# Eight attention blocks and two gated MLPs on one core: the weight conversions of block 0 regrouped into pairs, with unread products ahead of it

## The chip, the cores and the metric

One core of one Trainium2 chip runs the whole program. The metric is device time in microseconds of one execution; the kernel before stands at 1517.81 us, the median of three runs (1516.03 to 1519.38).

## The reference

```python
def sm_attn(qq, kk, vv):                      # q, k, v: (8, 8, 576, 64); p: (8, 8, 32, 64)
    s = scale * np.matmul(qq, kk.transpose(0, 1, 3, 2))
    a = np.exp(s - np.max(s, axis=-1, keepdims=True))
    a = a / (np.sum(a, axis=-1, keepdims=True) + 1e-09)
    return np.matmul(a, vv)
p_packed = sm_attn(p, k, v)
x = sm_attn(q, p_packed, p_packed)            # -> (4608, 512), heads side by side
h = x @ w_in;   x = (h / (1 + exp(-h))) @ w_out
h = x @ w_in2;  out = (h * clip(h + 3, 0, 6) / 6) @ w_out2
```

All eight batch entries pass through both MLPs with 2048 hidden features. The four weight matrices arrive as float64.

## The kernel before, in words

**Blocks.** The first MLP runs in nine blocks of 512 tokens (`block`, L840): one for the first 512 rows of each batch entry, and a ninth (`j == B`) for the eight tails of 64 rows. Block j computes MLP 1 for its tokens, and beside it the attention of entry j+1. For 16 groups f of 128 hidden features `hidden` (L788) issues 6 products of 512 columns (operands in a high and a low half: high by high, high by low, low by high), then a Silu on ACT (L814), a copy of the high half on ACT (L821) and the low half on DVE (L822). `projects` (L853) issues 12 products of group f-2. So a block has 288 products, 18 per group. The second MLP follows, over five stretches of tokens; the change does not touch it.

**Fused input weights.** In blocks 0 to 7 the attention output is not formed: `fuse_products` (L580) multiplies the packed values by the input weights `wi[g]`, four groups f at a time, and `fuse_split` (L586) makes the halves on ACT (L590) and DVE (L593). `hidden` multiplies these by the turned attention weights (`high_u` L538, `low_u` L543). The tails' rows are formed apart: `step_ut` (L554) turns the weights of the tail on DVE and spreads them on POOL (L560), `step_xt` (L564) multiplies, `flush` stores.

**Float64 conversion.** The weights of the first MLP come in 32 units of 128 rows by 512 numbers, 16 of `w_in` and 16 of `w_out`, each a load of 512 KB (`load_raw`, L117). A unit costs ACT two scalings (`conv_a` L142, `conv_b` L148), DVE a shift and a sign step (L157, L161) and POOL an add (L171 or L173). Units of `w_out` also get a high half on ACT (L184) and a low half on DVE (L189); the odd ones are stored (`keep`, L176) and read again in later blocks. Class `Feed` (L1265) sets the order: four units ahead of block 0, two begun there, the others at two calls of `advance` per group f. Inside block 0 the loads are issued from ACT's queue, before that from SP's.

**Order around it.** Everything ahead of block 0 is written out by hand (L1338 to L1457): loads, attention of entry 0, its first units, the first fused products. Inside the blocks the class `Plan` (L600) places the steps of `attention` (L746): its clock `now` counts products, plus a cost for each step; a step runs when its place (share of the block's products) is reached, when the steps it needs are a given number of counts old (times 1.5 in block 0) and when banks of PSUM are free. `plan.finish` (L669) runs what is left over at once: at the start of a group that needs fused weights, at `boundary` (L1504, after product 264 of 288) and at the block's end. Each engine takes its instructions in program order.

Of the kernel before, what the change touches and what calls it, by code (L numbers as in the profile page):

```python
# [18 lines left out]
def tile_pack_attention_two_mlps(ctx: ExitStack, tc, q, k, v, p, w_in1, w_out1, w_in2, w_out2, out):  # L19
# [5 lines left out]
    P = 128  # L25
# [9 lines left out]
    RAW = 6  # L35
# [12 lines left out]
    gp = opened(first_left, "gp", bufs=3)  # L48
# [68 lines left out]
    def load_raw(key):  # L117
        if key[0] == "in":
            _, g, c = key
            src = w_in1.bitcast(I32)[c * P:(c + 1) * P, 2 * g * T:2 * (g + 1) * T]  # L120
        else:
            src = w_out1.bitcast(I32)[key[1] * P:(key[1] + 1) * P, :]
        raw = cv.tile([P, 2 * T], I32, tag="raw", name="raw", bufs=RAW)
        (load_queue[0] if early[0] else nc.scalar).dma_start(out=raw, in_=src)
        raws[key] = raw
# [10 lines left out]
    def ring():  # L136
        return cv.tile([P, T], F32, tag="ring", name="cr", bufs=8)

    def conv_a(key, room=ring):
        raw = raws.pop(key).rearrange("p (f t) -> p f t", t=2)  # L140
        r = room()
        nc.scalar.mul(out=r, in_=f32(raw[:, :, 1]), mul=2.0 ** -112)  # L142
        raws[key] = raw, r.bitcast(I32)

    def conv_b(key, room=ring):
        raw, r = raws.pop(key)
        t = room().bitcast(I32) if room is ring else raw[:, :, 0]
        nc.scalar.mul(out=t, in_=raw[:, :, 0].bitcast(U32), mul=2.0 ** -29)  # L148
        raws[key] = raw[:, :, 1], r, t
# [18 lines left out]
    def conv_add(key):  # L168
        r, t = raws.pop(key)
        if key[0] == "in":  # L170
            nc.gpsimd.tensor_add(out=wi[key[1]][:, key[2], :].bitcast(I32), in0=r, in1=t)  # L171
            return
# [3 lines left out]
    def keep(behind=2):  # L176

        while len(kept) > behind:
# [3 lines left out]
    def conv_hi(key):  # L182
        v, w = raws[key], half_w(key[1])
        nc.scalar.copy(out=w[:, 0], in_=v)  # L184
        made[key] = w

    def conv_lo(key):
        f, v, w = key[1], raws.pop(key), made[key]
        nc.vector.tensor_sub(out=w[:, 1], in0=v, in1=f32(w[:, 0]))  # L189
        if f % 2:  # L190
            kept.append((w1o[f].rearrange("n p f -> p n f"), f32(w)))

    def conv_end(key):
        conv_hi(key)
        conv_lo(key)
# [31 lines left out]
    class Prep:  # L227
# [31 lines left out]
        def all(self):  # L259
# [3 lines left out]
            for u, (kind, f, h) in enumerate(self.units):  # L263
                key = "p", u
                c = self.pool.tile([P, 8, P], F32, tag="c8", name="c8", bufs=2)
# [61 lines left out]
    def load_nat(b, what, c):  # L327
# [3 lines left out]
        if what == "v":  # L331
# [20 lines left out]
    def load_next():  # L352

        while loaded[0] < min(used[0] + 6, len(uses)):
# [18 lines left out]
    def turn(b, what, c, engine):  # L373
# [7 lines left out]
        turn_rows(ps, m)  # L381
# [171 lines left out]

    def step_ut(b):  # L554
# [31 lines left out]
    def fuse_split(b, g, to):  # L586
# [974 lines left out]
```

## Time and profile before

| | |
|---|---|
| median of three runs | 1517.81 us |
| the profiled execution | 1516.45 us, span 1514.7 us |
| TensorE (PE) busy, granted clock over the span | 1454.8 us (96%), 0.985 |
| DVE, ACT, POOL busy | 1011.8, 736.0, 187.3 us |
| first product of block 0 / of a projection / of block 1 | 43.04 / 59.74 / 172.90 us |
| DMA | 316.56 MB, mean 209 GB/s |

Busy times of matrix products overlap, since they are pipelined; starts in the timeline are the surer measure. A line `A <- B` in the view of waits says that A's engine sat idle and that B ended it.

### The profile page before, as it was taken

The numbers are of one execution on the slowest core, as the hardware profiler recorded it, in microseconds if no ns is written. First come the engines' busy times: TensorE is split into PE (matmuls) and PEld (weight loads), VectorE is DVE, ScalarE is ACT, GpSimd is POOL, SyncE is SP. The second block draws the span as 40 slices with busy tenths as digits, with TensorE's granted clock in tenths as the row PEclk, the third lists the DMA queues.
The fourth block names the chain that finished last, engine by engine and source line by source line (L and its number), as shares of the span: only waits on it lengthen the run. The fifth ranks groups of instructions, "written<-read, shape, count | busy, mean of one in ns | idle before, by whom it ended". The sixth has DMA issues, their size and how long they took to land.

```text
span 1514.7 us, 21753 instructions
## 1 busy us (share of the span) xinstructions
PE 1454.8 (96%) x7860; PEld 1167.6 (77%) x7860; DVE 1011.8 (67%) x1590; ACT 736.0 (49%) x1146; POOL 187.3 (12%) x150
## 2 busy tenths in 40 slices
PE   6688699999999999999999999999999999999998
PEld 3456467777777777777888888888888888999998
DVE  5666546565655655543682769786978687778767
ACT  4676346545465646545662344334443443444443
POOL 1333011111111121123240000000000000000000
PEclk9899899999999999999999999999999999999999
DMA  9567376857576576468983566577657766998887
GB/s 227 181 189 193 101 221 189 218 150 213 141 214 177 164 177 188 129 178 225 296 254 122 192 218 219 194 222 248 222 195 221 237 216 211 284 313 253 273 273 221
DMA packets 394186, 316.56 MB, mean 209 GB/s; under 512 B 189280, under 2 KB 291168, under 8 KB 393568
## 3 DMA queue, kind: packets, MB, share of 16 engines
q1 hardware_dynamic: 386328, 300.56, 67.6%
q10 hardware_dynamic: 7752, 14.62, 3.1%
q8 instruction: 63, 1.03, 0.3%
q14 instruction: 43, 0.35, 0.1%
HBM read 257.43 MB, written 57.67 MB: 208 GB/s over the span
## 4 chain that ended last, share of the span: by engine, by line
PE 86%; ACT 5%; DVE 4%; DMA 2%; issue 1%; POOL 1%; SPq 1%; ACTq 0%; POOLq 0%; DVEq 0%
PE acc L829 8%; PE b L1087 8%; PE b L1085 8%; PE b L1086 8%; PE b L1180 8%; PE b L1183 7%; PE acc L831 7%; PE b L1182 7%; PE acc L830 7%; PE hps L802 4%; PE hps L804 4%; PE hps L803 4%; PE abank L406 3%; DMA nat<-in_k_dram 1%; ACT hps L814 1%
## 5 line engine op out<-in xcount | busy, mean ns | idle before, releaser
L822 DVE TENSOR_TENSOR gl<-hps,gh 128x512 fp32r<-128x512 f32 x144 | 99.1, 688 | 221.3 <-ACT gh L821 221.1
L1183 PE MATMUL b<-ro,ws 128*128 128x512 f32 (+2 forms) x564 | 206.2, 366 | 0.0
L1182 PE MATMUL b<-ro,ws 128*128 128x512 f32 (+2 forms) x564 | 206.2, 366 | 0.0
L1085 PE MATMUL b<-xc,ws 128*128 128x512 f32 (+1 forms) x560 | 205.8, 367 | 0.0
L1087 PE MATMUL b<-xc,ws 128*128 128x512 f32 (+1 forms) x560 | 205.6, 367 | 0.0
L1086 PE MATMUL b<-xc,ws 128*128 128x512 f32 (+1 forms) x560 | 205.6, 367 | 0.0
L1128 DVE TENSOR_TENSOR ro<-g,ro 128x1024 fp32r<-128x1024 f32 (+1 forms) x140 | 161.2, 1156 | 42.1 <-ACT ro L1123 41.7
L1123 ACT CAST ro<-g 128x1024 fp32r<-128x1024 f32 (+1 forms) x140 | 131.8, 965 | 94.0 <-DVE g L1116 33.4
L814 ACT ACTIVATE hps<-hps 128x512 f32<-128x512 f32 x144 | 84.0, 584 | 154.4 <-PE hps L804 153.9
L1180 PE MATMUL b<-ro,ws 128*128 128x512 f32 (+2 forms) x564 | 139.0, 367 | 0.3
L829 PE MATMUL acc<-gh,wr 128*128 128x512 f32 x288 | 117.0, 406 | 8.0 <-ACT wr L184 8.0
L829 PE MATMUL acc<-gh,wo 128*128 128x512 f32 x288 | 117.2, 407 | 3.1 <-DMA wo<-w1o 3.0
L1183 PEld LDWEIGHTS b<-ro,ws 128*128 128x128 f32 x564 | 105.9, 188 | 13.2
L1182 PEld LDWEIGHTS b<-ro,ws 128*128 128x128 f32 x564 | 105.9, 188 | 13.1
L1085 PEld LDWEIGHTS b<-xc,ws 128*128 128x128 f32 x560 | 105.1, 188 | 13.5
L1086 PEld LDWEIGHTS b<-xc,ws 128*128 128x128 f32 x560 | 105.1, 188 | 13.2
L1087 PEld LDWEIGHTS b<-xc,ws 128*128 128x128 f32 x560 | 105.1, 188 | 13.1
L1180 PEld LDWEIGHTS b<-ro,ws 128*128 128x128 f32 x564 | 102.9, 188 | 15.1 <-DVE ro L1128 2.1
L802 PE MATMUL hps<-a2h,fused 128*128 128x512 f32 x256 | 107.0, 418 | 7.3 <-ACT fused L590 7.3
L831 PE MATMUL acc<-gh,wo 128*128 128x512 f32 x288 | 114.0, 396 | 0.1
L831 PE MATMUL acc<-gh,wr 128*128 128x512 f32 x288 | 113.5, 394 | 0.4 <-DVE wr L189 0.4
L830 PE MATMUL acc<-gl,wo 128*128 128x512 f32 x288 | 113.2, 393 | 0.0
(173 smaller groups left out, 2653.9 us busy)
## 6 DMA issues: line engine op xcount, KB each, us to landing
ws<-w2in SPq DMA_DIRECT2D x280, 256.0 KB, 3.2
ws<-w2out SPq DMA_DIRECT2D x280, 256.0 KB, 3.0
wo<-w1o SPq DMA_DIRECT2D x64, 512.0 KB, 4.5
x1d<-x SPq DMA_DIRECT2D x18, 512.0 KB, 3.8
praw<-in_moe_w_in_dram SPq DMA_DIRECT2D x32, 256.0 KB, 4.5
praw<-in_moe_w_out_dram SPq DMA_DIRECT2D x32, 256.0 KB, 4.5
raw<-in_moe_w_out_dram ACTq DMA_DIRECT2D x15, 512.0 KB, 3.6
nat<-in_v_dram SPq DMA_DIRECT2D x28, 256.0 KB, 3.2
```

Source lines behind the costliest of these rows:

```text
L802: mm(ps, lhsT=wh, rhs=rh, start=c == 0, stop=False)
L829: mm(acc[e], lhsT=w[:, 0, s], rhs=gh, start=first, stop=False)
L830: mm(acc[e], lhsT=w[:, 0, s], rhs=gl, start=False, stop=False)
L831: mm(acc[e], lhsT=w[:, 1, s], rhs=gh, start=False, stop=last)
L1085: mm(ps, lhsT=wh, rhs=xs[k][:, 0, c], start=first, stop=False, skip_group_check=True)
L1086: mm(ps, lhsT=wh, rhs=xs[k][:, 1, c], start=False, stop=False, skip_group_check=True)
L1087: mm(ps, lhsT=wl, rhs=xs[k][:, 0, c], start=False, stop=last, skip_group_check=True)
L1123: nc.scalar.copy(out=t[:, 0], in_=v)
L1128: nc.vector.tensor_sub(out=t[:, 1], in0=self.operand(s), in1=f32(t[:, 0]))
L1180: mm(to, lhsT=wh, rhs=x, start=False, stop=last, skip_group_check=True)
L1182: mm(to, lhsT=wh, rhs=x, start=first, stop=False, skip_group_check=True)
L1183: mm(to, lhsT=wl, rhs=x, start=False, stop=False, skip_group_check=True)
```

## The change

The diff below is cut; a line of "..." stands for lines left out.

1. Conversion units are taken in pairs (`raw` and `ring` tiles twice as wide, three `raw` buffers in place of six), so 16 pairs in place of 32 units; halves are still made one unit at a time. The loads go out on SP's queue throughout.
2. `Feed` gets a table: pair k starts at step `STARTS[k]`; its scalings, shift, sign, add and halves follow at steps +0, +1, +3, +4, +6, +9, +11, and at +6 the next load is asked for. Inside block 0 a step passes every 4.5 products. Steps below zero are issued ahead of block 0. The first loads of entry 1 move from ahead of block 0 to steps 1 to 9.
3. Ahead of block 0 the order is rewritten: entry 0's q is loaded ahead of v, in long rows, and turned by ordinary products; the softmax of the second attention takes the tail with it; 9, 8 and 20 products of 128 columns whose result nobody reads stand at three places (four of 512 columns before).
4. `attention`: waits are longer, `u` is cut in three steps, `exps` steps run only right after a group's Silu, `s` needs the `ut` of the entry before. At the end of blocks 0 to 5 `ut`, `xt` and `flush` may stay open into the next block. In block 0 places p become 0.1 + 0.84 p.

```diff
-    RAW = 6
+    RAW = 3
     def load_raw(key):
+        raw = cv.tile([P, 2, 2 * T], I32, tag="raw", name="raw", bufs=RAW)
+        for i in range(2):
...
-        (load_queue[0] if early[0] else nc.scalar).dma_start(out=raw, in_=src)
+            nc.sync.dma_start(out=raw[:, i], in_=src)
     def ring():
-        return cv.tile([P, T], F32, tag="ring", name="cr", bufs=8)
+        return cv.tile([P, 2, T], F32, tag="ring", name="cr", bufs=4)
+    def ring_low():
+        return gp.tile([P, 2, T], F32, tag="x1", name="ct", bufs=2)
...
     def turn(b, what, c, engine):
-        turn_rows(ps, m)
+        if b or what == "k":
+            turn_rows(ps, m)
+        else:
+            for i in range(NI):
+                for h in range(2):
+                    mm(ps[h * D:(h + 1) * D, i * P:(i + 1) * P], lhsT=m[:, h, i, :], rhs=ident, start=True, stop=True)
...
         def ready(self, key, need, tile, bank, count):
-            if key[0] == "exps" and not self.calm:
+            if key[0].startswith("exps") and not self.calm:
...
         add("s", 0.17, 6, lambda: step_s(b), ("kp", 7), (last, 7), bank=9, count=3)
+        steps[-1][4].append((("ut", b - 1), 0))
...
-            add(f"exps{e}", 0.17, 0, lambda e=e: exp1(b, e), (f"max{e}", 6))
-        add("t", 0.3, 6, lambda: step_t(b), ("exps1", 10), bank=8, count=3)
-        add("pp", 0.4, 9, lambda: step_pp(b), ("t", 9), ("post1", 0), bank=6)
-        add("pt", 0.45, 3, lambda: step_pt(b), ("pp", 7), bank=7)
-        add("z", 0.52, 6, lambda: step_z(b), ("pt", 8), (last, 7), bank=12, count=3)
+            add(f"exps{e}", 0.17, 0, lambda e=e: exp1(b, e), (f"max{e}", 8 + 2 * e))
+        add("t", 0.3, 6, lambda: step_t(b), ("exps1", 13), bank=8, count=3)
+        add("pp", 0.4, 9, lambda: step_pp(b), ("t", 11), ("post1", 0), bank=6)
+        add("pt", 0.45, 3, lambda: step_pt(b), ("pp", 11), bank=7)
+        add("z", 0.5, 6, lambda: step_z(b), ("pt", 12), (last, 7), bank=12, count=3)
...
-        add("ut", 0.75, 0, lambda: step_ut(b), ("post21", 8))
-        add("xt", 0.8, 2, lambda: step_xt(b), ("ut", 12), bank=6)
+        add("ux", 0.65, 0, lambda: turn_u(b, 0), ("post20", 14), bank=24)
+        add("uh", 0.65, 0, lambda: high_u(b, 0, st["u", b, 0]), ("ux", 8))
+        add("ul", 0.65, 0, lambda: low_u(b, 0, st.pop(("u", b, 0))), ("uh", 8))
+        add("ut", 0.7, 0, lambda: step_ut(b), ("post21", 10))
+        add("xt", 0.75, 2, lambda: step_xt(b), ("ut", 16), bank=6)
...
     def block(j, nxt, boundary):
+            while j == 0 and feed.at <= at_[0] / 4.5:
+                feed.advance()
...
         def projects(f, between=None):
+            if j == 0:
+                feed.need(("out", f // 2))
...
-        plan.finish()
+        plan.finish(lambda key: key[0] not in ("ut", "xt", "flush") or j >= B - 2)
...
     class Feed:
+            order = [(0, 0), (0, 1), 0, (1, 0), (1, 1), 1, 2, (2, 0), (2, 1), 3, 4, (3, 0), (3, 1), 5, 6, 7]
+        def plan(self):
+            self.steps, self.ready = {}, set(self.keys[:2])
+            for first, key in zip(STARTS, self.keys[2:]):
+                todo = [(0, conv_a), (1, conv_b), (3, conv_shift), (4, conv_sign), (6, conv_add)]
+                if key[0] == "out":
+                    todo += [(9, conv_hi), (11, conv_lo)]
...
+                self.steps.setdefault(first + 6, []).append((20, lambda: self.load()))
+                if key[0] == "out":
+                    self.steps.setdefault(first + 15, []).append((21, keep))
...
+    FILL = (9, 10, 8, 20)
+    STARTS = (-9, -6, -2, 1, 6, 9, 12, 15, 20, 24, 28, 31, 37, 42)
+    LOADS = [(1, lambda: load_p(1)), (1, lambda: load_tail(1, "k"))]
+    LOADS += [(2 + i, lambda i=i: load_next(i + 1)) for i in range(6)]
+    LOADS += [(8, lambda: load_tail(1, "v")), (9, lambda: load_tail(1, "q"))]
...
+    def fill(count):
+        for _ in range(count):
+            mm(filler[:, 0:P], lhsT=ident, rhs=ident, start=True, stop=True)
+    fill(FILL[0])
...
+    exp2(*SOFT2[0])
+    ending(unit[0])
+    feed.load()
+    beginning(unit[1])
...
+    ending(unit[1])
+    feed.load()
+    fill(FILL[2])
+    to = fuse_products(0, 0)
+    fill(FILL[3])
     turn_on(AF.Silu)
+    feed.advance()
+    feed.advance()
+    made_ = fuse_high(0, 0, to)
...
+    turn_u(0, 0)
+    high_u(0, 0, st["u", 0, 0])
+    fuse_low(0, 0, to, made_)
+    low_u(0, 0, st["u", 0, 0])
+    turn_u(0, 1)
...
+    while feed.at < 0:
+        feed.advance()
...
         def boundary(j=j):
-                plan.finish(lambda key: key == ("post21", j + 1))
+                plan.finish(lambda key: key in (("post21", j + 1), ("ul", j + 1)))
```

## Rows read from the trace of the kernel before

**Rows 1.** Windows, three stages: length, busy of PE, PEld, DVE, ACT, POOL, clock, DMA, GB/s.
```profile
43.04:59.74 16.70, 8.73 (x31) 6.44 (x31) 6.92 (x15) 11.69 (x19) 2.81 (x2) 0.70 0.58 175
59.74:172.90 113.16, 89.91 (x509) 61.05 (x510) 74.80 (x135) 72.46 (x121) 39.41 (x28) 0.90 0.57 167
337.60:417.50 79.90, 79.90 (x507) 58.41 (x506) 47.48 (x93) 43.54 (x73) 13.96 (x12) 1.00 0.64 168
```

**Rows 2.** Waits of PE from 59.74 to 172.9: us in total, times, longest.
```profile
PE abank L567 <- POOL tails L560: 11.0, 1, 11.0
PE acc L829 <- ACT wr L184: 8.0, 1, 8.0
PE hps L802 <- ACT fused L590: 6.7, 2, 3.8
PE abank L406 <- DVE gl L822: 2.6, 1, 2.6
PE hps L804 <- DVE fused L593: 1.4, 2, 0.8
```

**Rows 3.** Waits of PE from 0 to 43.04, ahead of block 0.
```profile
PE abank L406 <- POOL wi L171: 5.3, 2, 3.4
PE abank L371 <- DMA nat<-in_q_dram: 2.4, 1, 2.4
```

**Rows 4.** Timeline of PE: start, length, what.
```profile
27.78 3.70 PE L1328 MATMUL unused<-wi,ident 128*128 128x512 f32 x8
...
163.47 0.63 PE L830 MATMUL acc<-gl,wo 128*128 128x512 f32 x1
163.90 0.63 PE L831 MATMUL acc<-gh,wo 128*128 128x512 f32 x1
...
172.68 0.39 PE L831 MATMUL acc<-gh,wo 128*128 128x512 f32 x1
172.90 0.40 PE L802 MATMUL hps<-a2h,fused 128*128 128x512 f32 x1
```

**Rows 5.** Lines by form: block 0 for 512 columns, later stages for 1024; busy, mean ns.
```profile
L161 DVE SCALAR_TENSOR_TENSOR cr<-raw,cr 128x512 int32<-128x512 int32 x28 | 18.0, 683 | 0.0
L157 DVE TENSOR_SCALAR cr<-cr 128x512 int32<-128x512 int32 x28 | 10.6, 419 | 0.0
L142 ACT ACTIVATE cr<-raw 128x512 f32<-128x512 f32 x28 | 18.9, 675 | 14.4 <-DVE cr L161 9.9 <-DMA raw<-in_moe_w_out_dram 4.5
L814 ACT ACT_TABLE_LOAD x4 | 5.1, 1283 | 1.9 <-PE hps L804 1.8
...
L986 ACT CAST xc<-xs 128x1024 fp32r<-128x1024 f32 x4 | 4.2, 1050 | 6.8 <-DVE xs L995 6.8
...
L1128 DVE TENSOR_TENSOR ro<-g,ro 128x1024 fp32r<-128x1024 f32 x84 | 106.2, 1267 | 28.4 <-ACT ro L1123 28.4
...
L1164 POOL TENSOR_TENSOR ov<-ov,o 128x1024 f32<-128x1024 f32 x3 | 7.2, 2404 | 422.8 <-ACT ov L1152 422.8
```

**Rows 6.** Timeline of DVE ahead of block 0.
```profile
27.05 0.72 DVE L498 STREAM_TRANSPOSE soft<-abank 128x512 f32<-128x512 f32 x1 [1.65 <-PE abank L406]
...
39.78 0.72 DVE L535 STREAM_TRANSPOSE abank<-soft 128x512 f32<-128x512 f32 x1
```

**Rows 7.** Timeline of DVE and POOL in block 0, alone and beside each other.
```profile
45.13 0.29 DVE L507 TENSOR_TENSOR soft<-soft,s2m 128x128 f32<-128x128 f32 x1
...
63.71 1.13 DVE L524 TENSOR_TENSOR soft<-soft,s2s 128x128 f32<-128x128 f32 x1
...
63.39 1.30 POOL L173 TENSOR_TENSOR cr<-cr 128x512 int32<-128x512 int32 x1
```

**Rows 8.** Line 124, the loads of raw units, and the stretch of one wait for them.
```profile
DMA to landing us min/median/max: 3.2/4.1/9.0
...
51.77:59.74 7.97, 0.00 (x1) 0.00 (x0) 2.29 (x6) 4.11 (x7) 2.81 (x2) 0.77 0.93 299
```

**Rows 9.** Waits of PE from 172.9 to 830, blocks 1 to 8.
```profile
PE acc L829 <- DMA wo<-w1o: 3.0, 1, 3.0
PE abank L567 <- POOL tails L560: 2.6, 3, 1.7
```

More of the change, by code (lines that the diff above doesn't have):

```diff
@@ L174, in conv_add, with keep @@
         raws[key] = f32(r)
-    def keep(behind=2):
-        while len(kept) > behind:
+    def keep():
+        while kept:
             to, w = kept.pop(0)
@@ L594, in fuse_split @@
             fused[b, g, e] = hi, lo
+    def fuse_split(b, g, to):
+        fuse_low(b, g, to, fuse_high(b, g, to))
     def fuse(b, g):
+        if b == 0:
+            for c in range(2):
+                feed.need(("in", g, c))
         fuse_split(b, g, fuse_products(b, g))
+    SLOW = 1.5
     class Plan:
@@ L1268, in __init__ @@
         def __init__(self):
[L1269 to L1282 removed]
+            order = [(0, 0), (0, 1), 0, (1, 0), (1, 1), 1, 2, (2, 0), (2, 1), 3, 4, (3, 0), (3, 1), 5, 6, 7]
+            self.keys = [("in", *k) if isinstance(k, tuple) else ("out", k) for k in order]
+            self.loaded = self.at = 0
         def load(self):
@@ L1287, in load @@
                 self.loaded += 1
-        def advance(self):
-            i, n = self.at, len(self.keys)
-            if i > n + 1:
-                keep(0)
-                return
-            for _ in range(2):
-                if self.loaded < i + self.ahead - (self.loaded == n - 1):
-                    self.load()
-            keep()
-            if self.ended < i - 1:
-                self.end()
-            if i < n and self.begun == i:
-                self.begin()
-            if i < n and i % 2:
-                for step in conv_shift, conv_sign, conv_add:
-                    for key in self.keys[i - 1:i + 1]:
-                        step(key)
+        def plan(self):
[4 more added lines that the diff above has]
+                    todo += [(9, conv_hi), (11, conv_lo)]
+                todo += [(todo[-1][0], self.ready.add)]
+                for off, fn in todo:
+                    self.steps.setdefault(first + off, []).append((off, lambda fn=fn, key=key: fn(key)))
+                self.steps.setdefault(first + 6, []).append((20, lambda: self.load()))
+                if key[0] == "out":
+                    self.steps.setdefault(first + 15, []).append((21, keep))
+            for first, fn in LOADS:
+                self.steps.setdefault(first, []).append((30, fn))
+            self.last = max(self.steps)
@@ L1307, in advance, with need @@
+        def advance(self):
+            for _, fn in sorted(self.steps.pop(self.at, []), key=lambda x: -x[0]):
+                fn()
             self.at += 1
+        def need(self, key):
+            while key not in self.ready:
+                self.advance()
         def end(self):
-            key = self.keys[self.ended]
-            if key[0] == "out":
-                conv_end(key)
-            self.ended += 1
-        def begin(self):
-            if self.begun <= self.at < len(self.keys) and self.begun < self.loaded:
-                conv_begin(self.keys[self.begun])
-                self.begun += 1
+            while self.at <= self.last:
+                self.advance()
@@ L1336, in tile_pack_attention_two_mlps @@
     unit = feed.keys
+    beside(load_p, 0)
     load_nat(0, "k", 0)
-    beside(load_p, 0)
-    beside(load_nat, 0, "k", 1)
+    load_nat(0, "k", 1)
     load_nat(0, "k", 2)
-    beside(load_nat, 0, "k", 3)
+    load_nat(0, "k", 3)
     load_tail(0, "k")
-    feed.load()
+    for c in range(HP):
+        load_nat(0, "q", c)
     for c in range(HP):
@@ L1462, in tile_pack_attention_two_mlps @@
             for key, place, cost, fn, need, held, count in attention(j + 1):
-                plan.add(key, place, cost, fn, need, None, held, count=count)
+                plan.add(key, place if j else 0.1 + 0.84 * place, cost, fn, need, None, held, count=count)
         if j < B:
@@ L1518, in tile_pack_attention_two_mlps @@
         if j == 0:
-            keep(0)
+            feed.end()
         if j == B:
```

224 lines of the change are left out of this document (92 added, 132 removed).

## The prediction, made before the changed kernel ran

> **What bounds the kernel now.** I read the busy table first: TensorE is 96% busy, so a gain can come only from stretches in which it is not. The windows by stage show where they are. A later block takes 79.9 us and is PE throughout, at the full clock; from the first projection product of block 0 (59.74) to the first product of block 1 (172.90) it is 113.16 us with 89.91 busy at a granted clock of 0.90, and the 16.7 us before that hold 8.73 [rows 1]. The waits of PE tell what ended the idle time: the spread tails of entry 1 (11.0), the first high half of the output weights (8.0, just ahead of 59.74), then the halves of the fused weights and their banks (6.7, 2.6, 1.4) [rows 2]. Ahead of block 0 PE waited for fused input weights to be converted (5.3) and for q (2.4) [rows 3]; but PE is no bound there, DVE is, from the first turned score to the turned weights u [rows 6]. After 172.9 there is little to win: 3.0 and 2.6 us [rows 9].
>
> So the case is the first 173 us. In the 113.16, 23.2 is idle (113.16 - 89.91). [...] Work alone is 113.2 - 23.2 - 5.6 = 84.4 us. The sum below is made against the profiled execution's 1516.45 us; the median of the runs is 1.36 above it.
>
> **Part A, up to the first projection product (59.74).** The unread products go to an engine that is not the bound. Four of 512 columns took 3.70 us [rows 4], so one of 128 columns is about 0.23, and 20 of them 4.6 us. They stand behind the first fused products and ahead of the first hidden product, while DVE still works on the softmax; what hides them is a wait for a load, worked out below, and without that cover up to 2.3 us of the 4.6 would show. The 9 and 8 lie in waits for loads and for conversions. I cost all three at nothing; their worth is a full clock at the first products, which that same wait undoes.
>
> q ahead of v, in one load for a head pair instead of two, ends the 2.4 us wait [rows 3]. SP now issues all eight k loads, which two queues shared, but the two unit loads that stood between k and q go behind. The turn of q costs more PE: eight products with two passes each where four transposes stood, bounded by 0 and 1.2 us for each q, half of it while PE waits for exp. I take the first score of the second attention 2.0 earlier, at 25.0; ends 0 and 3.5.
>
> From there DVE needed 39.78 - 27.05 = 12.7 us to the turning of u [rows 6], with the conversion of three units in it. Now two pairs are in it: by the 1024-wide rows 1.27 for a sign step and 0.7 for a shift, 3.9 for both pairs, where three units at 0.68 + 0.42 are 3.3 [rows 5]. The tail adds a fifth to four operations, and one multiplication comes from POOL to DVE. Against that, POOL's adds stretched the old steps. I keep 12.7: u is turned at 37.7, against 39.78.
>
> What then sets the first projection is ACT's queue. `conv_a` of the second output pair is issued at step 1, ahead of the Silu of group 0, and its load leaves only after the sign step of the first output pair, which waits behind DVE's turn, two low halves of fused weights, low half, second turn and second low half, plus one copy on ACT between: 0.72 + 1.29 + 0.69 + 0.72 + 0.58 + 0.69, then 0.67 + 1.27, 6.6 us (512 columns on DVE at 0.69 to 0.72 [rows 5, 6], the copy a little under a scaling's 0.675). A load of 512 KB landed after 4.1 us (3.2 to 9.0), and two took turns at 299 GB/s [rows 8], so 1.75 more for the second half: 5.9. Then a scaling of 1.05 by the cast of this width [rows 5], Silu and copy at 0.59: 2.2. Together 14.7, so the first projection product comes at 52.4. Part A gives 7.3; bounds 0.5 (no gain at q, a load of 9.0 + 1.75) and 10.5.
>
> Queued behind that waiting `conv_a` are Silu and high halves of groups 0 to 2; PE runs three groups ahead and then waits, some 6 us in place of 8.0. This wait is not removed, it has a new place.
>
> **Part B, from there to block 1 (113.2).** Work is 84.4; the first two steps of entry 1 come in behind the first projection (+1.1), the tails' product can go into block 1 (-0.6): 84.9.
>
> Conversions: 28 units were left in block 0's stretch, now 11 pairs and a few halves. A pair saves ACT two fixed costs of some 0.1 each and 26 issues of DMAs leave its queue. The engines keep up: ACT 72.46 and DVE 74.80 of 113 us busy [rows 1]; the same work less a few us would be some 80% of 90 us. SP takes the loads; behind a load that waits for its buffer stand the stores of halves and the loads of entries 1 and 2, asked for five or more steps ahead. A pair is asked for 3 to 7 steps ahead of its scaling, a step being 4.5 products or some 1.3 us, against a landing of 5.9: the pair with 3 steps and some others come late by 1 to 2 us. PE notices only what exceeds the 4 us (18 products at 0.22) by which Silu runs ahead of the projection. I take 2; ends 0 and 8.
>
> Fused weights: the planner still runs two of the three groups at the last moment, at products 48 and 120, and the third three products ahead (by its arithmetic: bank and place conditions, times 1.5). So the wait for the first halves stays. The three waits were 0.8, 5.5 (2.6 and 2.9) and 4.4 (3.8 and 0.6) [rows 2]; in the second ACT had just loaded tables. `exps` steps now stand behind the group, so I take 2 each, 6, and 2 for the clock: 8, ends 3 (0.8 each) and 17.
>
> The boundary: by the same arithmetic z runs at product 234, the two maxima steps at 249 and 255; the exponentials need 18 counts more and a moment right after a Silu, the last of which is at 252. So they fall to `finish` at 264, with everything up to u. What hides this chain is 24 products, 5.5 us. It is a table load of 1.28 [rows 5], an exp of 0.6, sum, reciprocal and product of the first piece 1.8, of the wider second 2.1, turn and copy 1.3 (all at 0.7 for 512 columns): 7.1, and the second half of u another 2.7 while PE has three products to do. This is what is late next, in place of the 11.0 us for the tails, which the larger distance and the leave to run over do away with. I take 3.1 and 1.4 for the clock: 4.5, ends 1 and 8.
>
> With 0.8 for the turned packed values and 1.4 for the clock at the start: 84.9 + 2 + 8 + 4.5 + 0.8 + 1.4 = 101.6. Part B gives 11.6.
>
> **Part C, later blocks.** Of the 2.6 us for tails some 0.5 stays (16 counts for 12), and the tails' product of entry 1 comes in: 1.5. The 3.0 for the first stored halves stays [rows 9]. The step `s` waits for the `ut` before it; that runs at product 279 of block 0, so nothing is held up.
>
> **Sum.** 1516.45 - 7.3 - 11.6 - 1.5 = 1496.0, with 1.4 to the median 1497.
>
> **A rule against it.** An add of POOL and a DVE operation beside it hold each other up: a 128-wide product took 1.13 us beside an add of 1.30, a subtraction of its size 0.29 alone [rows 7]. A pair's add should take 2.40 [rows 5], so one meeting costs up to 2.4. [...] If each of 12 adds in block 0 puts half its length, 1.2, on the path, 14 us go, and the time is 1511. Against it: POOL was busy 39 us after 59.74 too, in halves of that size.
>
> **Rivals.** (1) The halves of the fused weights and the boundary find free queues: their lower ends, 3 and 1, and no late pair, instead of 8, 4.5 and 2, give 10.5 more: 1486. For it: 0.8 us was all that the first group cost. Chance 0.2. (2) The adds' hold, 1511, chance 0.1. (3) Slower: the loads lose their lead. Three buffers let a load leave only when DVE has signed the pair three before; `conv_a` ahead of the Silu then stops ACT, that the low halves on DVE, those the next sign step, and each pair pays its landing anew. It decides from some 1.9 us a pair on PE (20.4 over 11 pairs), a landing of about 11 us where 4 steps and 4 us of slack cover 9. At 3.5 us a pair the time is 1497 + 38 = 1535. For it: ACT already waited 4.5 us for loads and 9.9 for tiles [rows 5]; against it: 299 GB/s in that wait and a longest landing of 9.0 [rows 8]. Chance 0.09. (4) The fillers and the new order do not act: the load takes its 10.8 and q gains nothing (part A 0.5), late pairs cost 6, fused groups 12, the boundary 8 (part B 113.1, a gain of 0.1): 1516.45 - 0.5 - 0.1 - 1.5 = 1514.4, with the median 1516, chance 0.05.
>
> **How the numbers follow.** The forecast has 0.56. A measurement of this kernel can tell 0.2%, 3 us. Faster: forecast, (1) and (2), 0.86; same: (4), 0.05; slower: (3), 0.09. The range takes in (1) with a part A 3 us better (1483) and (2) (1512), and leaves out (3), (4) and some of the ends.
>
> **What would show it.** Right: the first projection product near 52 with a wait of some 6 us for a copy behind `conv_a`, that one waiting for a raw load; block 1 near 154; the wait for tails gone or under 1 us, a new one of 2 to 4 us for a2h or a2l at block 1's start; three waits of 1 to 4 for fused halves; later blocks at 80. Wrong: PE idle over 5 us inside block 0 after its start, raw loads landing after 9 us, DVE operations of over 2 us beside POOL in series, or a block 1 that starts its scores late.

## The result and the profile after

The changed kernel takes 1496.22 us (median of 4 runs, 1494.75 to 1497.99) against 1516.92 (4 runs, 1513.61 to 1519.38) for the kernel before in the same series: a ratio of 0.9865, 95% interval 0.9842 to 0.9889. The profiled execution took 1495.15 us with a span of 1493.3, 21.4 less than before. The prediction was 1497.0 (1483 to 1512).

**Where it went.** Windows of the changed kernel, from its first projection product to the first product of block 1, as in [rows 1], and from there to the last product of block 1: length, busy time of PE, PEld, DVE, ACT and POOL, granted clock, DMA share, GB/s.

```profile
51.72:148.05 96.33, 86.48 (x518) 60.53 (x519) 67.12 (x101) 61.76 (x91) 31.41 (x13) 0.95 0.73 206
148.05:232.33 84.28, 81.78 (x500) 57.66 (x501) 47.22 (x94) 43.89 (x72) 12.78 (x11) 0.98 0.74 212
```

The first projection product comes at 51.72 instead of 59.74: 8.0 us gained. From there to block 1 it is 96.33 us instead of 113.16: 16.8 gained. PE's idle time in this stretch fell from 23.2 us to 96.33 - 86.48 = 9.9, and its clock rose from 0.90 to 0.95. From block 1 to the end it is 1493.3 - 148.05 = 1345.25 against 1514.7 - 172.90 = 1341.8: 3.45 lost. The sum is 21.4.

Waits of PE in that stretch of the changed kernel, to set beside [rows 2]: us in total, times, longest.

```profile
PE acc L859 <- ACT gh L851: 3.9, 1, 3.9
PE hps L832 <- ACT fused L604: 3.1, 2, 2.4
PE abank L462 <- ACT T L93: 2.3, 1, 2.3
PE abank L417 <- ACT T L93: 2.1, 1, 2.1
PE hps L834 <- DVE fused L610: 0.9, 1, 0.9
```

The 3.9 lies just ahead of 51.72, as the 8.0 lay ahead of 59.74. The 11.0 for the tails is gone, the fused halves fell from 6.7 to 3.1. New are two short waits for T, turned operands of entry 1 that ACT copies out of PSUM. Four of the five lie in the stretch and sum to 8.4; with a wait of 1.45 at its end, shown below at 148.05, they are the 9.9.

Why PE waits less is seen on ACT, which converts. Waits of ACT in block 0's stretch, the longest of the kernel before (59.74 to 172.9) and then of the changed one (51.72 to 148.05):

```profile
ACT cr L142 <- DVE cr L161: 9.9, 7, 2.4
ACT wr L184 <- POOL cr L173: 9.0, 5, 3.8
```

```profile
ACT fused L604 <- PE abank L417: 8.1, 2, 5.3
ACT cr L148 <- DMA raw<-in_moe_w_in_dram: 6.3, 1, 6.3
ACT wr L192 <- POOL cr L179: 4.7, 3, 1.8
```

Before, the next scaling stood seven times at the head of ACT's queue until DVE had signed an older unit (9.9), and the high half until POOL had added (9.0). With the written steps each operation is issued when its input is nearly there: no wait for the sign step, 4.7 for the add. In their place one load is late (6.3).

**Ahead of block 0.** DVE's timeline, as in [rows 6], with two of POOL's adds: start, length, what.

```profile
23.45 0.72 DVE L509 STREAM_TRANSPOSE soft<-abank 128x512 f32<-128x512 f32 x1 [0.23 <-PE abank L417]
...
27.39 0.91 DVE L509 STREAM_TRANSPOSE soft<-abank 128x512 f32<-128x512 f32 x2
28.33 0.82 DVE L514 TENSOR_REDUCE s2m<-soft 128x20 f32<-128x640 f32 x1
29.19 1.48 DVE L518 TENSOR_TENSOR soft<-soft,s2m 128x640 f32<-128x640 f32 x1
...
33.16 1.92 DVE L530 TENSOR_SCALAR s2s<-s2s 128x16 f32<-128x16 f32 x1
...
38.12 0.72 DVE L546 STREAM_TRANSPOSE abank<-soft 128x512 f32<-128x512 f32 x1
...
45.07 3.32 DVE L167 SCALAR_TENSOR_TENSOR cr<-raw,cr 128x1024 int32<-128x1024 int32 x1
...
27.63 2.35 POOL L177 TENSOR_TENSOR wi<-cr,ct 128x1024 int32<-128x1024 int32 x1 [25.40 <-DVE cr L167]
32.67 2.37 POOL L177 TENSOR_TENSOR wi<-cr,ct 128x1024 int32<-128x1024 int32 x1 [2.69 <-DVE cr L167]
44.58 2.73 POOL L179 TENSOR_TENSOR cr<-cr,ct 128x1024 int32<-128x1024 int32 x1 [9.54 <-DVE cr L167]
```

The first turned score is at 23.45 (before 27.05) and u turns at 38.12 (before 39.78). In between stand two operations that POOL's add stretched: 1.48 where the later 640-wide product takes 0.83, 1.92 where the 20-column sister takes 0.18. The kernel before has such operations there too; they are shown further down.

ACT's timeline ahead of the first projection, and PE's around it:

```profile
47.34 1.16 ACT L154 ACTIVATE ct<-raw 128x1024 int32<-128x1024 uint32 x1 [2.31 <-POOL cr L179]
48.37 0.63 ACT L192 CAST wr<-cr 128x512 fp32r<-128x512 f32 x1
48.88 0.64 ACT L192 CAST wo<-cr 128x512 fp32r<-128x512 f32 x1
49.40 1.16 ACT L148 ACTIVATE cr<-raw 128x1024 f32<-128x1024 f32 x1
50.42 0.63 ACT L844 ACTIVATE hps<-hps 128x512 f32<-128x512 f32 x1
51.08 0.59 ACT L851 CAST gh<-hps 128x512 fp32r<-128x512 f32 x1
```

```profile
36.95 6.69 PE L1393 MATMUL unused<-ident 128*128 128x128 f32 x40
43.40 0.48 PE L832 MATMUL hps<-a2h,fused 128*128 128x512 f32 x1
...
51.72 0.79 PE L859 MATMUL acc<-gh,wr 128*128 128x512 f32 x1 [3.94 <-ACT gh L851]
...
148.05 0.50 PE L832 MATMUL hps<-a2h,fused 128*128 128x512 f32 x1 [1.45 <-ACT a2h L551]
```

ACT's low scaling waits 2.3 us for POOL to release the buffer of the low parts (two of them); the high halves, a scaling, Silu and the copy follow without a gap.

**Behind block 0**, waits of PE from 155 to 830, to set beside [rows 9]:

```profile
PE abank L581 <- POOL tails L574: 2.4, 4, 1.0
PE acc L859 <- DMA wo<-w1o: 1.1, 1, 1.1
```

### The profile page after: what moved, and what is told of

The parts are those of the page before. It is cut to its first block, busy times and chain, and to the rows that moved or that the text cites. A ratio compares the mean times of both kernels' runs of the same rounds, so it can differ in the third digit from the quotient of the medians.

```text
span 1493.3 us, 21861 instructions
## 1 busy us (share of the span) xinstructions
PE 1456.3 (98%) x7974; PEld 1173.9 (79%) x7974; DVE 1009.0 (68%) x1555; ACT 724.7 (49%) x1107; POOL 180.6 (12%) x133
## 4 chain that ended last, share of the span: by engine, by line
PE 87%; ACT 5%; DVE 4%; DMA 1%; issue 1%; POOL 1%; SPq 0%; POOLq 0%; DVEq 0%; ACTq 0%
PE acc L859 8%; PE b L1121 8%; PE b L1123 8%; PE b L1122 8%; PE b L1216 8%; PE b L1219 7%; PE b L1218 7%; PE acc L861 7%; PE acc L860 7%; PE hps L832 5%; PE hps L834 4%; PE hps L833 4%; PE abank L417 3%; ACT soft L446 1%; ACT hps L844 1%
## 5 line engine op out<-in xcount | busy, mean ns | idle before, releaser
L1218 PEld LDWEIGHTS b<-ro,ws 128*128 128x128 f32 x564 | 105.9, 188 | 13.1
L1219 PEld LDWEIGHTS b<-ro,ws 128*128 128x128 f32 x564 | 105.9, 188 | 13.1
L1122 PEld LDWEIGHTS b<-xc,ws 128*128 128x128 f32 x560 | 105.1, 188 | 13.1
L1123 PEld LDWEIGHTS b<-xc,ws 128*128 128x128 f32 x560 | 105.1, 188 | 13.1
L860 PE MATMUL acc<-gl,wr 128*128 128x512 f32 x288 | 114.1, 396 | 0.2 <-DVE gl L852 0.2
```

What stands on the lines that cost most here:

```text
L860: mm(acc[e], lhsT=w[:, 0, s], rhs=gl, start=False, stop=False)
L1122: mm(ps, lhsT=wh, rhs=xs[k][:, 1, c], start=False, stop=False, skip_group_check=True)
L1123: mm(ps, lhsT=wl, rhs=xs[k][:, 0, c], start=False, stop=last, skip_group_check=True)
L1218: mm(to, lhsT=wh, rhs=x, start=first, stop=False, skip_group_check=True)
L1219: mm(to, lhsT=wl, rhs=x, start=False, stop=False, skip_group_check=True)
```

## The experiments

Each is an edit of the changed kernel. A ratio is to the kernel before in the same series: runs 1, 2, 4 and 5 are one series, 3, 6, 7 and 8 another, 9 to 12 a third. The changed kernel gave 0.9865 in the section above and 0.9870 in run 12; a ratio's interval is some 0.0015 to either side, 2.3 us.

**The theory from the profile after:** part A is worth what q's place in the load order is worth, and ends in ACT's queue; part B comes from the places of the conversions, since ACT no longer blocks; fillers and wide operations only accompany it. Rivals: the fillers' clock, the wide operations' saved fixed costs, the planner's distances.

**1. No fillers.**

```diff
-    FILL = (9, 10, 8, 20)
+    FILL = (0, 0, 0, 0)
```

> All 37 unread products are left out. Theory (the queue of ACT sets the first projection): in the changed kernel the first hidden product stands behind the 20 fillers, which end at 43.40, while its operand was ready near 39.5; yet PE then waits 3.94 us for the high half of group 0, which ACT makes at 51.08 whatever PE does. So the first hidden product comes near 40 to 41, the first projection stays at 51 to 52.5, and the time is that of the changed kernel, 1496 within 2 us. [...] Rival 2 (the fillers hold PE up): the 3.9 us come through: 1492 to 1493.

1497.85 us, ratio 0.9872 (0.9855 to 0.9888). The first hidden product came at 40.74 instead of 43.40, and PE waited 3.98 for gh all the same. So the 20 fillers hide in ACT's queue, as costed. The first hidden products started 0.43 apart up to 47.01, against 0.23 with fillers, and the wait took that back. The first score came at 24.67 and the first projection at 52.89, both 1.2 later. In the runs that leave the order up to there alone (4 to 8 and 10 to 12) the first score lies between 22.92 and 23.75, so the profile gives the 9 fillers at the start about 1 us; the ratio is too coarse to show it.

**2. q last.** The loads of q go behind v, v's tail and a raw pair, about where they stood before.

```diff
     load_tail(0, "k")
-    for c in range(HP):
-        load_nat(0, "q", c)
     for c in range(HP):
         load_nat(0, "v", c)
     load_tail(0, "v")
-    load_tail(0, "q")
     feed.load()
+    for c in range(HP):
+        load_nat(0, "q", c)
+    load_tail(0, "q")
```

> The loads of entry 0's q go behind v, the tail of v and the first raw pair, as in the kernel before; their long rows and the turn by products stay. Theory (the early q moved the second attention): the first score of the second attention, at 23.45 in the changed kernel and 27.05 before, comes 1.5 to 3 us later, a wait of PE for q appears, and the first projection is 1 to 3 us later: 1497 to 1499. Rival (it is the k loads and the two unit loads taken out from between that moved it): q is still in time, 23.5 to 24, and the time stays within 1 us of 1496.

1504.67 us, ratio 0.9917 (0.9902 to 0.9932). PE's waits, its first projection, and DVE's first score and turn of u:

```profile
PE abank L392 <- DMA nat<-in_q_dram: 6.3, 1, 6.3
...
59.81 0.80 PE L859 MATMUL acc<-gh,wr 128*128 128x512 f32 x1 [4.23 <-ACT gh L851]
...
31.59 0.72 DVE L509 STREAM_TRANSPOSE soft<-abank 128x512 f32<-128x512 f32 x1 [0.23 <-PE abank L417]
...
46.26 0.72 DVE L546 STREAM_TRANSPOSE abank<-soft 128x512 f32<-128x512 f32 x1
```

First score, u and first projection all move by 8.1 us, and the time by 0.9917 - 0.9865, some 8 us: this chain is passed on one to one. The turns of q show what the 8.1 consists of. The products that read the loaded q, in the changed kernel and then in this one: ns of one (least, median, most), first and last start in us.

```profile
L392 PE MATMUL abank<-ident,nat x32: 272/273/323, 12.8 to 14.5; 128*64 128x128 f32 x32
```

```profile
L392 PE MATMUL abank<-ident,nat x32: 421/421/474, 19.4 to 22.6; 128*64 128x128 f32 x32
...
20.00:25.00 5.00, 5.00 (x48) 4.34 (x46) 1.54 (x4) 0.58 (x1) 0.00 (x0) 0.54 1.03 340
```

The first starts 6.6 us later and the last 8.1: behind the wait the clock was granted at 0.54 from 20 to 25, so each took 0.42 instead of 0.27. The kernel before had as many raw bytes ahead of q, in two units, one ahead of v, and turned its first q tile at 18.41, 5.6 later than the changed kernel; its first score was 3.6 later. So 8.1 is more than the kernel before paid; it turned q by four transposes a tile, between other products.

**3. q behind v alone**, to part q's place from the pair's.

```diff
     for c in range(HP):
-        load_nat(0, "q", c)
-    for c in range(HP):
         load_nat(0, "v", c)
+    for c in range(HP):
+        load_nat(0, "q", c)
```

> q goes behind v only; the tails and all raw pairs come after it. Theory (the 8 us that q cost behind v and a pair were the bytes in front of it, 2 MB at some 280 GB/s, 7 us): v alone is 1 MB, 3.5 us, of which some 2 are hidden by the first softmax; a wait of PE for q of 1.5 to 3 us, the first score of the second attention 1.5 to 3 later, 1498 to 1500. Rival (the order against v is nothing, the raw pair was all): no wait for q, within 1 us of 1496.

1498.48 us, ratio 0.9860 (0.9843 to 0.9876). PE waits 2.0 us for q, the first score comes at 24.55 and the first projection at 52.84, both 1.1 later; as in run 1 that is more than the other runs differ by and too little for the ratio. So what costs most in the run above is the raw pair ahead of q with the clock behind the wait; v alone costs about 1.

**4. The tails' product may not run over**, as in the kernel before.

```diff
-        plan.finish(lambda key: key[0] not in ("ut", "xt", "flush") or j >= B - 2)
+        plan.finish()
```

> ut, xt and flush must end within their block again (the full finish); nothing else is undone. Theory (the 11.0 us went because the queues of DVE and ACT are no longer late, and only the product of entry 1 runs over): one wait for spread tails of 1 to 2.5 us at the end of block 0, the later blocks as they are, 1496 to 1499. Rival (the leave to run over is what removed the 11.0): a wait of 6 us or more for tails in block 0, 1502 or later.

1499.08 us, ratio 0.9879 (0.9864 to 0.9894), span 1498.0. The wait came back at half its old size:

```profile
154.02 1.12 PE L581 MATMUL abank<-tails,pp 128*64 128x256 f32 x4 [5.54 <-POOL tails L574]
```

Before it was 11.0 [rows 2]. So of the 11.0 about half went by the rest of the change, the larger distances and earlier places among it, the other half by the leave to run over. What the leave is worth in time is less sure: the span says 4.7 us, or 1.7 against the second profile of the changed kernel (run 12), and the ratios differ by 0.0014, 2 us, which is within their intervals.

**5. Raw loads of block 0 from ACT's queue**, where the kernel before had them.

```diff
-            nc.sync.dma_start(out=raw[:, i], in_=src)
+            (nc.sync if early[0] else nc.scalar).dma_start(out=raw[:, i], in_=src)
```

> Inside block 0 the loads of raw pairs are issued from ACT's queue, as before; pairs, places and everything else stay. Theory (the move to SP took waits out of ACT's way): SP waited 35 us in all for the sign steps of DVE before such loads, up to 11 at once, and on ACT these stand ahead of Silu and high halves: ACT is blocked at several loads, PE waits for Silu or high halves by 5 to 15 us more, 1501 to 1511. Rival (by the time a load is issued its buffer is free, 2 steps after the sign, and both queues feed the same engines): within 2 us of 1496, or faster, since ACT's loads no longer stand behind entry 1's loads on SP.

1500.72 us, ratio 0.9890 (0.9875 to 0.9904): some 4 us, below what was expected, with an interval that touches that of the changed kernel. The waits of PE show where a blocked ACT is felt, at the fused halves (3.1 before the edit) and at gh:

```profile
PE hps L832 <- ACT fused L604: 9.9, 2, 7.9
PE acc L859 <- ACT gh L851: 6.0, 1, 6.0
```

**6. The exponentials of the second softmax at any step**, as the kernel before allowed.

```diff
-            if key[0].startswith("exps") and not self.calm:
+            if key[0] == "exps" and not self.calm:
```

> The exponentials of the attention may run at any step again, not only right after a group's Silu; distances and places stay. Theory (their place behind the Silu is what keeps ACT free for the fused halves and the Silu): in block 0 the exponentials come earlier and apart, more table loads fall between, PE waits for fused halves or Silu by 2 to 4 us more, 1498 to 1501; the exponentials of the second softmax no longer fall to the boundary, so the wait for a2h there (1.45 us) goes. Rival (the place does nothing, the distances do): within 1 us of 1496, or 2 us faster by the boundary.

1495.54 us, ratio 0.9846 (0.9831 to 0.9861). Nothing is lost. Block 1 started at 146.70, without the wait for a2h that the changed kernel has at 148.05, and from 157 to 840 the tails' waits gave way to six waits for softmax weights, 5.3 us. In the two profiles what is saved at the boundary is spent inside the blocks.

**7. Old distances and places from block 1 on**, with old freedom for the exponentials and the tails kept inside those blocks.

```diff
+        new = b < 2
+        pick = lambda a, c: a if new else c
...
-        add("z", 0.5, 6, lambda: step_z(b), ("pt", 12), (last, 7), bank=12, count=3)
+        add("z", pick(0.5, 0.52), 6, lambda: step_z(b), ("pt", pick(12, 8)), (last, 7), bank=12, count=3)
...
-        plan.finish(lambda key: key[0] not in ("ut", "xt", "flush") or j >= B - 2)
+        plan.finish(lambda key: key[0] not in ("ut", "xt", "flush") or j >= 1)
```

> From block 1 on the attention steps have the distances, places and free exponentials of the kernel before, and tails must end in their block; block 0 stays as changed. From block 1 on the changed kernel took 3.4 us longer than the kernel before. Theory (that is block 0's boundary reaching over: late operands and the lower clock at block 1's start): later blocks take what they took, the time stays within 1 us of 1496. Rival (the longer distances in blocks 1 to 6 cost it, a few tenths a block): 1493 to 1495.

1496.02 us, ratio 0.9849 (0.9834 to 0.9864), span 1495.7: in sum the later blocks neither gain nor lose. From block 1's start (150.56) to the end it is 1345.1 us, as in the changed kernel. But two effects cancel in it: blocks 2 to 5 take 319.9 us, where the changed kernel takes 322.5, and block 6 takes 83.31 against 80.58, as PE waits 1.7 for the tails there and its clock is granted at 0.98.

**8. Eighteen more unread products in the wait for gh.** In the changed kernel PE waits 3.94 us there, and the 12 products behind the wait take 5.75 us from start to start (51.72 to 57.47), the later of them 0.43 apart with the clock granted at 0.50. At 0.23 apart, as the hidden products ahead of the wait run, they would take some 2.75, by the author's estimate. The run asks whether unread products in the wait gain these 3 us, and whether block 0 ends earlier by them.

```diff
+            if j == 0 and f == lag:
+                for _ in range(18):
+                    mm(acc[KC - 1][:, 0:P], lhsT=ident, rhs=ident, start=True, stop=True)
             if f >= lag:
```

> 18 more unread products of 128 columns stand ahead of the first projection of block 0, in the bank whose accumulation begins there. [...] Rival (what is late behind the wait is ACT, and PE runs into the next wait by what it gained): no change, 1496, with a longer wait for the fused halves of the second group.

1495.8 us, ratio 0.9852 (0.9836 to 0.9867). PE's timeline:

```profile
46.55 4.18 PE L912 MATMUL acc<-ident 128*128 128x128 f32 x36
51.77 0.49 PE L859 MATMUL acc<-gh,wr 128*128 128x512 f32 x1 [1.04 <-ACT gh L851]
```

The first projection comes at 51.77, as without the edit, and its products start closer (every third product 0.70 apart, where the changed kernel has 1.28), so 12 of them end some 2 us earlier. Yet block 1 starts at 148.59, not earlier, and the wait for the fused halves grows from 3.1 to 5.4. At this place the clock has no worth that shows: PE gets 2 us earlier to the next wait for ACT, and waits 2.3 longer.

**9. Pairs loaded, but converted by halves.** Each of the five operations is issued twice, for 512 columns.

```diff
+    def halves(pair):
+        return [(slice(None), i) for i in range(2)] if pair else [slice(None)]
+
...
-        nc.scalar.mul(out=r, in_=f32(raw[..., 1]), mul=2.0 ** -112)
+        for i in halves(room is ring):
+            nc.scalar.mul(out=r[i], in_=f32(raw[..., 1][i]), mul=2.0 ** -112)
```

> The changed kernel with its pair loads, steps and places kept, but each of the five conversion operations issued as two halves of 512 columns, as the kernel before had them. Theory (the gain of block 0 comes from the places and from what no longer waits, not from the wide operations): ACT pays 0.3 us more for each scaling (0.68 twice against 1.05), DVE's two pairs ahead of block 0 some 0.3 to 0.6 in all, so the first projection comes 0.5 to 2 us later and block 0 stays within 2 us: ratio to the kernel before 0.986 to 0.989. Rival 1 (the wide operations carry it: fewer fixed costs on ACT): 6 us and more, ratio above 0.990. Rival 2 (the pair add of 2.4 us on POOL holds DVE, and halves would hold it for less at a time): the turned weights u come 1 us earlier, not later than 37.2, and the ratio is below 0.985.

1497.03 us, ratio 0.9871 (0.9856 to 0.9885), against 0.9870 for the changed kernel beside it. First projection at 51.46 with u turned at 37.96, block 1 at 149.21. The wide operations as such have no worth that shows here: two halves of a sign step together took DVE 1.29 us, the wide one 1.22. From the first score (24.06) to u it took 13.90 instead of 14.67, since the halves of POOL's add held DVE for less, as the second rival says; in the time this does not show. That leaves the places and the order as what carries the gain, by elimination and not by a run of their own.

**10. q and v of entry 1 later.** The late load of 6.3 us had two explanations. SP's queue in the changed kernel, from 60 us on, shows one of them: the load that stopped ACT at 73.80 was issued only at 67.30, behind a store and seven small loads.

```profile
59.94 2.37 SPq L185 DMA_DIRECT2D w1o<-wo  x1
...
64.55 2.65 SPq L351 DMA_DIRECT2D nat<-in_q_dram  x4
67.30 1.03 SPq L126 DMA_DIRECT2D raw<-in_moe_w_in_dram  x2
```

The other is the DMA engines themselves, almost saturated there (window 84 to 96 of the changed kernel, columns as above):

```profile
84.00:96.00 12.00, 11.29 (x82) 7.50 (x68) 11.51 (x18) 9.69 (x15) 5.10 (x3) 1.00 0.99 346
```

```diff
-    LOADS += [(2 + i, lambda i=i: load_next(i + 1)) for i in range(6)]
+    LOADS += [(2 + i, lambda i=i: load_next(i + 1)) for i in range(4)]
+    LOADS += [(11, lambda: (cap.__setitem__(0, 1000), load_next()))]
...
+    cap = [4]
...
-        while loaded[0] < min(used[0] + 6, len(uses), most):
+        while loaded[0] < min(used[0] + 6, len(uses), most, cap[0]):
```

> The loads of q and v of entry 1 leave SP's queue from conversion step 11 instead of steps 6 to 9, so that nothing but k and the small loads of entry 1 stands ahead of the third input group's raw loads. Theory (SP issues without a break from 44.5 to 79 us, about 0.6 us for each load, and the raw load that stopped ACT for 6.3 us at 73.8 was issued only at 67.3): that raw load is issued some 4 us earlier, ACT waits 1 to 4 us instead of 6.3, and the time falls by 0 to 2 us, ratio 0.985 to 0.987. Rival 1 (the bandwidth is what lacks, the DMA engines are 0.95 to 0.99 busy from 52 to 96): ACT's wait stays above 5 and the time with it. Rival 2: q of entry 1 now comes late and TensorE waits for it, 1 to 5 us, ratio above 0.988.

1497.35 us, ratio 0.9871 (0.9856 to 0.9886). The load left at 63.09, 4.2 us earlier, and its wait shrank, but ACT met another:

```profile
ACT cr L148 <- DMA raw<-in_moe_w_out_dram: 4.5, 1, 4.5
...
ACT cr L148 <- DMA raw<-in_moe_w_in_dram: 4.1, 2, 2.5
```

8.6 us of waits for loads in place of 7.9 in the changed kernel beside it (6.3 and 1.6), no time gained. SP's order decides which load is late, not how late they are in sum; that fits the rival, bandwidth, but no run took bytes away.

**11. Runs 6, 8 and 10 together.**

> Three edits at once: q and v of entry 1 later as in the run before it, the exponentials of the second softmax at any step, 18 unread products ahead of the first projection. Theory: the exponentials take 1.5 us off block 1's start, the unread products bring 12 products to the full clock but the wait for fused halves behind them takes that back, the loads give 0 to 2: ratio 0.983 to 0.986, 1 to 3 us below the changed kernel of the same call. Rival: the same as the changed kernel within 1 us, since the work of ACT, DVE and the loads sets block 0 up to 112 us.

1494.52 us (4 runs, 1492.48 to 1496.2), ratio 0.9860 (0.9843 to 0.9876), span 1490.7: the best median of this series, 2.3 us below the run that follows, but the intervals overlap. It is not shown to be faster.

**12. The changed kernel again.**

> The changed kernel itself once more, beside the three others on the same chip: 1495 to 1498 us, ratio 0.985 to 0.988 by every theory.

1496.78 us, ratio 0.9870 (0.9856 to 0.9885). Its profiled execution spans 1496.3 us, 3 more than the first, and shows how much a single profile may be read for: block 1 starts at 149.85, as the clock was granted at 0.86 from 84 to 96 and at 0.96 from 112 on, where the first had 1.00.

```profile
51.61:149.85 98.24, 88.89 (x519) 62.35 (x519) 67.20 (x101) 61.83 (x91) 31.40 (x13) 0.92 0.73 202
```

Parts of one or two us ahead of block 1 are within this. Blocks 2 to 5 agree better: 322.50 us in the first profile, 322.43 in this one.

## Why the prediction was right, and where its steps were off

The total, the bounding engine and the two main gains stood; the split between the parts and four mechanisms did not. That the total came within 1 us is in part luck: part B came out 5.2 better than forecast and part C 5.0 worse, for the most part for reasons that have nothing to do with each other.

**q, the first term of part A.** Priced at 2.0, first score at 25.0; measured 3.6, 23.45, at the prediction's upper end of 3.5. The step that failed put the price on PE's 2.4 us wait [rows 3] less the added products. That wait was the end of a chain, and the two raw units that stood ahead of q were charged at nothing: with a pair there the order costs 8.1 (run 2), with v alone in front of q 1.1 (run 3).

**From the first score to u.** Kept at 12.7, measured 38.12 - 23.45 = 14.67. The working set the added work (two pairs for three units, "the tail adds a fifth", one multiplication from POOL) against "POOL's adds stretched the old steps" and let them cancel. They don't, because POOL stretches the new steps as much. In the kernel before three operations of this stretch were held:

```profile
32.90 1.45 DVE L161 SCALAR_TENSOR_TENSOR cr<-raw,cr 128x512 int32<-128x512 int32 x1
34.72 1.63 DVE L161 SCALAR_TENSOR_TENSOR cr<-raw,cr 128x512 int32<-128x512 int32 x1
36.98 0.81 DVE L519 TENSOR_SCALAR s2s<-s2s 128x16 f32<-128x16 f32 x1
```

Alone they take 0.69, 0.69 and 0.17, so the holds cost 2.3. In the changed kernel two operations cost 0.65 and some 1.7 more than their sisters alone, 2.4. The stretch is longer by 1.97 because of the added work, which the working had counted and set off: taken from start to start, 0.6 for the pairs and the rest for the tail and the multiplication. So more than q gave beyond its price was lost here: u turned 0.4 behind the forecast.

**The first projection.** Forecast 52.4, measured 51.72, by the right engine and queue but the wrong releaser. From u to there it was 19.96 us before and 13.60 now: 6.4 of part A's 8.0 were gained here, where ACT had stood 4.2 us for a raw load at 54.97. The step said that the scaling ahead of Silu waits for a load, 5.9 us after the sign step. No load was late there: it left at 44.50, as costed, and ACT's line at 49.40 has no wait. ACT waited 2.3 at 47.34 for POOL's add, because only two buffers hold the low parts, and ran four operations ahead of Silu where the sum had one. The diff had the two buffers in plain sight (`ring_low`, 2 of them); the working looked at the three raw buffers only. The "wait of some 6 us" was 3.9. That the fillers hide in the wait was right (run 1).

**Part B**, forecast 11.6, measured 16.8. No run shows the 5.6 us that "work alone" takes off for the clock; what the trace of the kernel before shows in its place is six, seven, seven and six products behind the starts at 59.74, 103.87, 135.13 and 162.88, 0.43 us apart and more with the clock granted at 0.50 to 0.53, where later ones start 0.23 apart: 1.2 to 1.9 us longer each, where the sums take 1.4, and some 5.9 in all. The fused halves were the term too large: 8 with the clock, where PE waited 3.1 + 0.9 and the clock fell behind the first wait only, granted at 0.72 from 67 to 73 and 1.00 from 73 to 148 (0.95 there in the repeated profile). The boundary, 4.5, lay only in part ahead of the cut: block 1's first product at 148.05 waits 1.45, and the clock comes behind it, granted at 0.79 from 148.05 to 156. The late load was right in kind: ACT lost 6.3 at 73.80. But PE ran on without a wait until 83.57, so the 2 us priced for it are not shown. The 0.8 for the turned packed values did not come. New and not foreseen were the two waits for T, 4.4 in all.

**Part C**, forecast a gain of 1.5, measured a loss of 3.45. Of that 1.3 is block 1 (84.28 against 82.96: the boundary's clock came in, while the wait for the first stored halves, kept at 3.0, fell to 1.1). Blocks 2 to 5 lose 2.4, windows before and after, columns as above:

```profile
257.70:577.77 320.07, 318.74 (x2018) 232.61 (x2016) 188.09 (x365) 174.60 (x290) 53.97 (x46) 1.00 0.69 179
234.17:556.67 322.50, 320.09 (x2018) 232.17 (x2016) 185.87 (x365) 173.72 (x290) 54.51 (x46) 1.00 0.69 178
```

This is no scatter: the stretch takes 322.4 to 322.5 in run 12 and in every run whose edit leaves later blocks alone, 322.4 without the tails' leave (run 4), 321.6 with the exponentials at any step (run 6), 319.9 with the old distances and places as well (run 7). So the longer distances and the exponentials' place cost 0.6 us a block, a term that the prediction put at nothing. Block 6 gives 1.1 back (80.58 against 81.69). The tails' waits did not shrink to 0.5: 2.4 against 2.6, now four where three stood. B and C together give 13.4 against a forecast of 13.1, but only the boundary is one cost on two sides of a cut.

**The rivals.** (1), free queues, had 22.1 for part B; the measured 16.8 lies halfway between that and the forecast's 11.6. (2), the hold by POOL's adds: it is real, but it is neither new (2.4 us up to u, 2.3 before) nor does it sum to 14. In block 0's stretch the largest holds on DVE were 1.9 (at 55.24), 1.3 (at 79.33) and 0.8 us (at 94.46), together 4 in 96; the kernel before has 1.0 (at 143.48), 0.8 (at 63.71) and 0.7 (at 152.56). (3), lost lead: seen once, 6.3 us on ACT; moving it (run 10) did not change the time. (4) is excluded by the ratio.

The first two of these three in DVE's timeline:

```profile
55.24 2.57 DVE L163 TENSOR_SCALAR cr<-cr 128x1024 int32<-128x1024 int32 x1
79.33 2.50 DVE L167 SCALAR_TENSOR_TENSOR cr<-raw,cr 128x1024 int32<-128x1024 int32 x1
```

**What the pieces are worth**, as far as the runs show: the order of the first loads 8.1 us if q goes behind a raw pair, though against the kernel before it moved the first score by 3.6 and u by 1.7; wide operations and fillers nothing that the time shows; the exponentials' place and the later distances a loss of 2.4 in blocks 2 to 5, which run 7 gets back there and loses again in block 6; the tails' leave some 2 to 5 us and raw loads off ACT's queue some 4, by profiles and medians whose intervals touch that of the changed kernel. What remains of the 21, the written steps of the conversions and with them the 6.4 from u to the first projection, was not undone alone, since the old order needs the old tiles and the old Feed. That they carry the rest is argued from ACT's waits (18.9 us for DVE's sign and POOL's add before, 4.7 after), not shown. That block 0 up to 112 us is now bound by the bytes of the weights is likewise only argued, from DMA shares of 0.88 to 0.99 and from runs 8 and 10.

## What to carry to other kernels

Price a load's place by the whole chain behind it and by every byte that goes ahead of it on its queue: the wait that the profile shows at its consumer is only the remainder (2.4 us shown, 3.6 gained, 8.1 lost when a raw pair was put in front again). An engine that converts data for others should get each operation when its input is ready (ACT stood 18.9 us behind the sign step and the add before, 4.7 after); count every ring of buffers on its path, the smallest first, and look at that engine's own waits, not at its busy share. Before a stretched operation is blamed for a loss, look for its like in the kernel before. And compare stages that repeat, block by block: they agree to 0.1 us here and show a loss that the medians hide.

## What the runs showed of the hardware

An add of POOL does not hold every operation of DVE. Beside the add from 27.63 to 29.98 two transposes (0.91) and a maximum over 640 columns (0.82) ran at their usual length, while the subtraction behind them took 1.48. Beside the one from 44.58 the sign step, 1.22 alone, took 3.32: the add's rest from 45.07 to 47.31 is 2.2, and 2.2 + 1.2 is 3.4. The shift at 44.35 had begun before the add and ran through in 0.69; that add took 2.73, where the two before it took 2.35 and 2.37. Of the held operations the subtraction and the sign step read two tiles, those at 33.16 and 55.24 one; no run shows what parts the held operations from the others. The prediction let each meeting with an add cost up to 2.4 us, whatever the operation.

Twice the width costs less than twice the time, on ACT and on DVE: a scaling of 1024 columns took 1.152 us (16 of them) against 0.675 for 512, the sign step 1.22 against 0.683. From start to start less is saved: two scalings of 512 took ACT 1.11 us in the kernel before (31.92 to 33.03) and 1.15 (43.84 to 44.99), one of 1024 in the changed kernel 1.06 (22.66 to 23.72) and 1.08 (41.74 to 42.82).

Unread products put into a wait of 4 us left the products behind it 0.23 apart instead of 0.43 (run 8), and the next wait took the time back: 5.4 us instead of 3.1.
